# Attention scores from zero-padded keys, earlier loads and another order at the start of a kernel

## The chip, the cores and the metric

The kernel runs on one core of one Trainium2 chip. The metric is the device time of one launch in microseconds; the median of three runs is given. One further execution was taken with the hardware profiler, and all rows below come from it. PE is TensorE (PEld its weight loads), DVE is VectorE, ACT is ScalarE, POOL is GpSimd, SP is SyncE, which issues nearly all of the DMAs.

## The reference

Attention in chunks is followed by two MLPs. All is float32.

```
for each chunk c of 32 queries (768 per sequence, 4 x 8 heads of size 64):
    keys = 8 memory keys + keys from 16 to the left to 8 to the right of the chunk
    a = softmax(q_c @ keys.T / 8);  out_c = a @ values        # 8 memory values likewise
x = out as (3072 tokens, 512)
h = x @ w_in;  g = where(h > 0, h, exp(min(h, 0)) - 1);  x = g @ w_out       # 512 -> 2048 -> 512
h = x @ w_in2; g = s * max(h, 0)**2 + b;                 out = g @ w_out2
```

## The kernel before

**Units.** Attention is cut into 24 units of 128 queries (4 chunks of 32) with all 8 heads. A unit loads `k` (512 KB, 128 partitions: rows 0 to 63 are the head dimension of one head of a pair, rows 64 to 127 that of the other), `q` (256 KB, laid out alike) and `v` (512 KB). A unit goes through these steps, named by a letter:

- S (`scores`, line 233): for each of 4 head pairs, 4 chunks and 2 heads one product of 64 rows, 32 columns of `q` against 64 keys of its head: 32 products, which the profile shows as 64 instructions, since each float32 product is issued twice. The two heads write two PSUM banks.
- M: on DVE the row maximum and the subtraction (lines 258, 259). E: the exponential on ACT (line 261). G: on DVE the sum, its reciprocal and the scaling (lines 263 to 266).
- P: four transposes on PE (line 281). T: their copy to `pt` on ACT (line 204).
- V (`values`, line 305): 32 products, shown as 64 instructions. X (`to_x`, line 317): ACT writes the rounded result to `xh` (line 204) and DVE the remainder to `xl` (line 208).

**MLP weights.** A chunk `raw` of w1 (512 KB) is loaded (line 149) and goes through four steps "w": ACT `top` (line 158), DVE `t` (line 161), ACT high part (line 172), DVE low part (line 208).

**The order at the start.** `EARLY` (line 39) is an order written out by hand for units 0 to 3 and the scores of unit 4. Each word is one step: S, M, E, G, P, T, V, X with the unit's number; `k` and `v` load a unit's `k` with `q`, or `v`; `l` loads a weight chunk; `w` is the next weight step; `d` are products without use; `h00` to `h11` are the first two halves of the products of weight chunks 0 and 1 with units 0 and 1. `keep` (line 130) chains the instructions of each engine in this order, so an engine does not pass over one that waits. SP issues its DMAs in program order too. After `EARLY` the main loop goes through the weight chunks, with the first MLP's products and the remaining attention units beside them; its first products (`h1`, line 386) need X of units 2 and 3.

**Memory.** `q`, `k` and `v` have two buffers each (`stg`, line 180), so the load of unit 2 waits until unit 0 has been used, and the load of unit 3 for unit 1. Scores of units 0 to 4 go through one pair of PSUM banks (`ps_a`, line 109).

Of the kernel before, what the change touches and what calls it, by code (L numbers as in the profile page):

```python
# [8 lines left out]
F32 = mybir.dt.float32  # L9
# [8 lines left out]
PSUM = bass.MemoryType.PSUM  # L18


B, H, S, D, NMEM = 4, 8, 768, 64, 8
CH, LEFT, RIGHT = 32, 16, 8
P = 128
DM, DFF, NT = H * D, 2048, B * S
KT, NF = DM // P, DFF // P
U = 4 * CH
# [3 lines left out]
NP = H // 2  # L30
# [6 lines left out]
NTOP = 1  # L37
LEAD = 4
EARLY = """
k1 l v0 k2 v1 k3 S0 M0 E0 d8 S1 G0 d2 P0 M1 w T0 w E1 S2 V0 w G1 l v2 k4 P1 M2 w X0 T1 E2 V1 G2 X1 S3 l v3 k5  # L40
P2 M3 w T2 w E3 h00 V2 w G3 h01 w X2 P3 l v4 T3 S4 h10 V3 w M4 E4 h11 w X3 G4 w w
"""
ORDER = (1, 2, 6, 5, 7, 3, 4)
BANK = {1: 1, 2: 2, 6: 1, 5: 5, 7: 1, 3: 5, 4: 1}
# [1 line left out]
NC, NCK = U // CH, LEFT + CH + RIGHT + NMEM  # L46
QC, KC, VC = NP * U, NC * NCK, NP * NC * D
# [14 lines left out]
def tile_attention_then_two_mlps(ctx, tc, q_in, k_in, v_in, w1, w2, s_in, b_in, out):  # L62
# [17 lines left out]
    nc = tc.nc  # L80
# [4 lines left out]
    def engine(step):  # L85
# [14 lines left out]
    wps = [ctx.enter_context(tc.tile_pool(name="wpi", bufs=1, side="right")),  # L100
           mctx.enter_context(tc.tile_pool(name="wpo", bufs=1))]
# [3 lines left out]
    xp = ctx.enter_context(tc.tile_pool(name="xp", bufs=1, side="right"))  # L105
# [4 lines left out]
    vctx = ExitStack()  # L110
    ps_v = vctx.enter_context(tc.tile_pool(name="ps_v", bufs=1, space=PSUM))
    xctx = ExitStack()
    ps_x = xctx.enter_context(tc.tile_pool(name="ps_x", bufs=1, space=PSUM))
    ps_acc = []

    y_dram = dp.tile([P, KT, NT], F32, name="y_dram")
# [13 lines left out]
    def keep(ins):  # L130

        if keeping[0]:
            e = ins.ins.engine
            if e in last:
                tc.add_manual_dep(ins.ins, last[e].ins.name,
                                  mybir.DependencyInfo(mybir.DependencyClass.NoSync, mybir.DependencyReason.DATA))
            last[e] = ins
        return ins
# [41 lines left out]
    stg = actx.enter_context(tc.tile_pool(name="stg", bufs=2))  # L180
# [6 lines left out]

    QK, V = {}, {}

    def load_qk(u):  # L190
        kb = stg.tile([P, NP, KC], F32, tag="k", name="kb")
        nc.sync.dma_start(out=kb, in_=k_in[u])
        q = stg.tile([P, QC], F32, tag="q", name="q")
        nc.sync.dma_start(out=q, in_=q_in[u])
        QK[u] = (q, kb)

    def load_v(u):
        V[u] = stg.tile([P, VC], F32, tag="v", name="v")
        nc.sync.dma_start(out=V[u], in_=v_in[u])

    def hi_copy(key, hi, src):
# [14 lines left out]
    def two_banks(nm):  # L216


        pool = ps_v if phase[0] == 0 and nm == "V" else ps_a
        return pool.tile([P, 2, 512], F32, tag="a", name="ps" + nm)  # L220
# [5 lines left out]
    def own_keys(u):  # L226

        return sms[u % 2].rearrange("p r z n -> p z r n")

    def by_halves(a):  # L230
        return a.rearrange("p (z r) -> p z r", z=2).unsqueeze(3).to_broadcast([U, 2, NP, NCK])

    def scores(u, ps):
        q, kb = QK[u]
        for r in range(NP):
            for c in range(NC):
                for z in range(2):
                    o, rows = slice(c * CH, (c + 1) * CH), slice(z * D, (z + 1) * D)
                    mm = keep(nc.tensor.matmul(ps[o, z, r * NCK:(r + 1) * NCK],
                                               q[rows, r * U + c * CH:r * U + (c + 1) * CH],  # L240
                                               kb[rows, r, c * NCK:(c + 1) * NCK], start=True, stop=True))
        return mm
# [5 lines left out]

    def softmax_steps(u, ps):

        src = ps[:, :, :NP * NCK].rearrange("p z (r n) -> p z r n", r=NP)
        sm, j = own_keys(u), u % UPB
        if j == 0:
            keep(nc.vector.memset(src[:CH, :, :, NMEM:NMEM + LEFT], NEG))
        if j == UPB - 1:
            keep(nc.vector.memset(src[U - CH:, :, :, NCK - RIGHT:], NEG))
        nmx, sums, rs = (ap2.tile([U, H], F32, tag=nm, name=nm) for nm in ("nmx", "sums", "rs"))
        keep(nc.vector.tensor_reduce(out=nmx.rearrange("p (z r) -> p z r", z=2), in_=src, op=ALU.max, axis=AX.X))
        keep(nc.vector.tensor_tensor(out=sm, in0=src, in1=by_halves(nmx), op=ALU.subtract))
        yield  # L260
        keep(nc.scalar.activation(out=sm, in_=sm, func=AF.Exp, scale=SCALE))
        yield
        keep(nc.vector.tensor_reduce(out=sums.rearrange("p (z r) -> p z r", z=2), in_=sm, op=ALU.add, axis=AX.X))
        keep(nc.vector.tensor_scalar(out=rs, in0=sums, scalar1=1e-9, scalar2=None, op0=ALU.add))
        keep(nc.vector.reciprocal(out=rs, in_=rs))
        keep(nc.vector.tensor_tensor(out=sm, in0=sm, in1=by_halves(rs), op=ALU.mult))
        yield

    def step_S(u):

        ps = two_banks("S")
        scores(u, ps)
        softmax(u, ps)

    def step_P(u):

        sm = sms[u % 2]
        if u < NU0:
            ps = (ps_h if ps_acc else ps_x).tile([P, 512], F32, tag="h", name="psP")
            for r in range(NP):  # L280
                keep(nc.tensor.transpose(ps[:, r * U:(r + 1) * U], sm[:, r].rearrange("p z n -> p (z n)"), ident))
            if keeping[0]:
                return ps
            return to_pt(ps)
        for c in range(NC):
            rows = slice(c * CH, (c + 1) * CH)
            for k in range(P // CH):
                z, n0 = divmod(k * CH, NCK)
                nc.vector.transpose(out=pt[k * CH:(k + 1) * CH, :, rows], in_=sm[rows, :, z, n0:n0 + CH])  # L289

    def to_pt(ps):

        keep(hi_copy("pt", pt, ps.rearrange("p (r n) -> p r n", r=NP)))
# [11 lines left out]
    def values(u, ps):  # L305
        v = V[u]
        for i in range(NP // 2):
            for c in range(NC):
                cs, o = slice(c * CH, (c + 1) * CH), 256 + i * U + c * CH
                for r in (2 * i, 2 * i + 1):  # L310
                    for z in range(2):
                        rows = slice(z * D, (z + 1) * D)
                        keep(nc.tensor.matmul(ps[r % 2 * D:(r % 2 + 1) * D, z, o:o + CH],  # L313
                                              v[rows, (r * NC + c) * D:(r * NC + c + 1) * D], pt[rows, r, cs],
                                              start=True, stop=True))

    def to_x(u, ps, behind=None):

        t, jj = tile_of[u]
        po = ps[:, :, 256:].rearrange("p z (i n) -> p z i n", i=NP // 2)  # L320
        if t < 2:
            if t not in X:
                X[t] = x_tiles(t)
            xh, xl = (x.rearrange("p (i z) n -> p z i n", z=2)[:, :, :, jj * U:(jj + 1) * U] for x in X[t])
            ins = keep(hi_copy("xh", xh, po)), keep(sub(xl, po, xh))
        else:
            xs = xsp.tile([P, KT, U], F32, tag="xs", name="xs")
            ins = (hi_copy("xh", xs.rearrange("p (i z) n -> p z i n", z=2), po),)
            nc.sync.dma_start(out=x_dram[:, :, u * U:(u + 1) * U], in_=xs)
        for i in ins if behind else ():  # L330
            wait(i, behind)
# [165 lines left out]
    load_qk(0)  # L497
    wraw = {}
    nc.vector.memset(pt, 1.0)
    for top in tops:  # L500
        nc.gpsimd.memset(top, 0)

# [34 lines left out]
    def weights_to(w, n, ahead):  # L537

        while wnext[0] < min(n, MICRO * NF):
            k, m = divmod(wnext[0], MICRO // 2)  # L540
            load_ws(w, k + 1 + ahead)
            if m == 0:
                wsteps[:] = [split_w(*SLOTS[k], wraw[k])]
            next(wsteps[0])
            wnext[0] += 1

    SM, PSV, PSP = {}, {}, {}

    def early(what):

        op_, n = what[0], int(what[1:] or 0)
        if op_ == "S":
            ps = two_banks("S")
            scores(n, ps)
            SM[n] = softmax_steps(n, ps)
        elif op_ in "MEG":
            next(SM[n])
        elif op_ == "P":
            PSP[n] = step_P(n)
        elif op_ == "T":  # L560
            to_pt(PSP.pop(n))
        elif op_ == "V":
            PSV[n] = two_banks("V")
            values(n, PSV[n])
        elif op_ == "X":
            to_x(n, PSV.pop(n))
        elif op_ == "w":
            weights_to(w1, wnext[0] + 1, 0)
        elif op_ == "d":
            warm(n)  # L570
        elif op_ == "h":
            h_half(*divmod(n, 10))
        elif op_ == "k":
            load_qk(n)
        elif op_ == "v":
            load_v(n)
        elif op_ == "l":
            load_ws(w1, wload[0] + 1)
# [167 lines left out]
    z = NTILE1 % 2  # L746
# [167 lines left out]
```

## Time and profile before

| | us |
|---|---|
| median of 3 runs | 1074.35 (1073.3 to 1074.74) |
| the profiled execution | 1074.13 |
| its span, first to last instruction | 1072.3 |

| engine | busy us | share of the span |
|---|---|---|
| PE | 1055.4 | 98% |
| PEld | 860.1 | 80% |
| DVE | 733.4 | 68% |
| ACT | 546.7 | 51% |
| POOL | 1.2 | 0% |

A matmul's end is modelled, so a busy PE need not be PE at its peak. The chain of waits is followed back from the last instruction; "issue" in it is time in which an engine waited for nothing that the profile shows. [...]

### The profile page before, as it was taken

The page shows a single profiled execution, that of the slowest core. Times are in us where ns is not written, and L with a number is a line of the kernel's source. Part 1 is how long each engine was busy: PE and PEld are TensorE (multiplying, and loading weights), DVE is VectorE, ACT ScalarE, POOL GpSimd, SP SyncE. Part 2 cuts the span into 40 slices and gives each one's busy share as a digit, 9 for nine tenths or more (in the row PEclk, how much of TensorE's full clock was granted, in tenths as well). Part 3 has the DMA queues.
Part 4 walks back from the last instruction along what each step waited for, and adds up shares of the span by engine and source line. Part 5 has one row for each costly group of instructions (what it writes and reads, how often), then busy time and mean ns, then how long its engine had stood idle before and what let it go on. Part 6 is the DMA issues. An engine that isn't in the chain of part 4 may idle for free.

```text
span 1072.3 us, 18728 instructions
## 1 busy us (share of the span) xinstructions
PE 1055.4 (98%) x7466; PEld 860.1 (80%) x7466; DVE 733.4 (68%) x1135; ACT 546.7 (51%) x771; POOL 1.2 (0%) x7
## 2 busy tenths in 40 slices
PE   7999999999999999999999999999999999999998
PEld 6778888888788888888888787788888788888886
DVE  6898677787777768778772356696266795375854
ACT  3777532434334367767653355654355653355542
POOL 0000000000000000000000000000000000000000
PEclk8999999999999999999999999999999999999999
DMA  8964214535234169988912566777766777766773
GB/s 322 394 259 193 92 60 135 174 104 177 73 119 143 37 208 341 343 329 322 330 59 79 170 192 188 230 213 234 233 190 188 243 214 232 210 189 195 204 201 126
DMA packets 94838, 213.02 MB, mean 199 GB/s; under 512 B 9760, under 2 KB 17952, under 8 KB 92704
## 3 DMA queue, kind: packets, MB, share of 16 engines
q1 hardware_dynamic: 94176, 210.79, 60.9%
q8 instruction: 59, 0.97, 0.4%
q10 hardware_dynamic: 576, 1.05, 0.3%
q14 instruction: 27, 0.22, 0.1%
HBM read 164.61 MB, written 47.19 MB: 198 GB/s over the span
## 4 chain that ended last, share of the span: by engine, by line
PE 83%; DVE 7%; DMA 5%; ACT 3%; issue 2%; SPq 0%; ACTq 0%; DVEq 0%
PE psH L361 14%; PE psH L363 13%; PE psH L362 13%; PE psL L362 7%; PE psL L363 7%; PE acc L361 6%; PE psL L361 6%; PE acc L362 6%; PE acc L363 6%; DMA hi<-y_dram 2%; DVE pt L289 2%; DMA xl<-x_dram 1%; DVE g L394 1%; PE psVS L313 1%; PE psV L313 1%
## 5 line engine op out<-in xcount | busy, mean ns | idle before, releaser
L361 PE MATMUL psH<-xh,w 128*128 128x512 f32 (+1 forms) x392 | 153.8, 392 | 0.8 <-DVE g L394 0.7
L362 PE MATMUL psH<-xl,w 128*128 128x512 f32 (+1 forms) x392 | 151.3, 386 | 0.6 <-issue 0.6
L363 PE MATMUL psH<-xh,w 128*128 128x512 f32 (+1 forms) x392 | 151.8, 387 | 0.0
L361 PE MATMUL acc<-gh,w 128*128 128x512 f32 x384 | 151.5, 395 | 0.0
L362 PE MATMUL acc<-gl,w 128*128 128x512 f32 x384 | 150.3, 391 | 0.0
L363 PE MATMUL acc<-gh,w 128*128 128x512 f32 x384 | 149.9, 390 | 0.0
L392 ACT ACTIVATE g<-psH 128x512 f32<-128x512 f32 x96 | 56.9, 593 | 99.6 <-PE psH L363 60.4
L394 DVE SCALAR_TENSOR_TENSOR g<-g,psH 128x512 f32<-128x512 f32 x96 | 65.7, 685 | 59.7 <-ACT g L393 58.5
L204 ACT ACTIVATE gh<-g 128x512 fp32r<-128x512 f32 x96 | 60.3, 628 | 77.7 <-DVE g L394 77.5
L361 PE MATMUL psH<-hi,hi 128*128 128x512 f32 x240 | 93.7, 397 | 0.8 <-ACT p L765 0.6
L363 PE MATMUL psH<-hi,hi 128*128 128x512 f32 x240 | 93.6, 390 | 0.0
L362 PE MATMUL psH<-hi,hi 128*128 128x512 f32 x240 | 93.5, 390 | 0.0
L815 ACT ACTIVATE g2xl<-g 128x1024 fp32r<-128x1024 f32 x56 | 59.5, 1062 | 60.1 <-PE psL L363 59.9
L362 PE MATMUL psL<-g2l,hi 128*128 128x512 f32 x224 | 87.4, 390 | 0.8 <-DVE g2l L208 0.7
L361 PE MATMUL psL<-g2xl,hi 128*128 128x512 f32 x224 | 86.9, 390 | 0.8 <-ACT g2xl L815 0.8
L361 PEld LDWEIGHTS psH<-xh,w 128*128 128x128 f32 x392 | 73.9, 188 | 17.0 <-DVE g L394 1.3
L363 PE MATMUL psL<-g2xl,hi 128*128 128x512 f32 x224 | 87.1, 389 | 0.0
L208 DVE TENSOR_TENSOR gl<-g,gh 128x512 fp32r<-128x512 f32 x96 | 66.2, 689 | 30.6 <-ACT gh L204 29.1
L362 PEld LDWEIGHTS psH<-xl,w 128*128 128x128 f32 x392 | 73.9, 189 | 16.0 <-issue 0.9
L363 PEld LDWEIGHTS psH<-xh,w 128*128 128x128 f32 x392 | 73.9, 188 | 15.5
L361 PEld LDWEIGHTS acc<-gh,w 128*128 128x128 f32 x384 | 72.1, 188 | 16.1
L363 PEld LDWEIGHTS acc<-gh,w 128*128 128x128 f32 x384 | 72.1, 188 | 15.6
(108 smaller groups left out, 1840.7 us busy)
## 6 DMA issues: line engine op xcount, KB each, us to landing
hi<-s_dram SPq DMA_DIRECT2D x336, 256.0 KB, 3.0
raw<-w SPq DMA_DIRECT2D x64, 511.8 KB, 6.3
s_dram<-right SPq DMA_DIRECT2D x16, 1024.0 KB, 5.1
kb<-k SPq DMA_DIRECT2D x24, 512.0 KB, 5.7
v<-v SPq DMA_DIRECT2D x24, 512.0 KB, 4.2
s_dram<-left SPq DMA_DIRECT2D x16, 768.0 KB, 4.1
q<-q SPq DMA_DIRECT2D x24, 256.0 KB, 5.2
out<-r SPq DMA_DIRECT2D x24, 256.0 KB, 3.7
```

The costliest lines, as they stand in the source:

```text
L204: return nc.scalar.activation(out=hi, in_=src, func=AF.Copy)
L208: return nc.vector.tensor_tensor(out=lo, in0=src, in1=f(hi), op=ALU.subtract)
L289: nc.vector.transpose(out=pt[k * CH:(k + 1) * CH, :, rows], in_=sm[rows, :, z, n0:n0 + CH])
L313: keep(nc.tensor.matmul(ps[r % 2 * D:(r % 2 + 1) * D, z, o:o + CH], v[rows, (r * NC + c) * D:(r * NC + c + 1) * D], pt[rows, r, cs], start ...
L361: keep(nc.tensor.matmul(o, sa(a[0]), sb(b[0]), start=first, stop=False, skip_group_check=again))
L362: keep(nc.tensor.matmul(o, sa(a[0]), sb(b[1]), start=False, stop=False, skip_group_check=again))
L363: return keep(nc.tensor.matmul(o, sa(a[1]), sb(b[0]), start=False, stop=last, skip_group_check=again))
L392: nc.scalar.activation(out=g[:, :n], in_=ps[:, :n], func=AF.Relu, scale=-1.0)
L394: nc.vector.scalar_tensor_tensor(out=g[:, :n], in0=g[:, :n], scalar=-1.0, in1=ps[:, :n], op0=ALU.add, op1=ALU.max)
L815: nc.scalar.activation(out=gh, in_=g[:, block], func=AF.Copy)
```

## The change

For units 0 to 3 the keys lie in a tile `WIDE` of twice the size: in its first half only the rows of the first head hold keys and the rows of the second are zero, in its second half the other way round. One product of 128 rows and 32 columns of `q` then gives both heads' scores, 128 columns wide: 16 products a unit instead of 32. The zeros are written once, by DVE for units 0 and 1 and by POOL for units 2 and 3, and `k` is loaded with two DMAs of 64 partitions (256 KB) each. `WIDE` uses the memory that `xh` and `xl` take later; `q` and `v` of units 2 and 3 use that of the last two weight chunks. Units 0 to 4 no longer share buffers of `k`; only `q` and `v` of units 4 and 5 (and `k` from unit 6 on) reuse earlier ones. The scores of units 0 to 3 alternate between two single banks. `EARLY` loads nearly everything first, has another order of steps, no `d`, and `k5 v4` at its end; both orders have 12 steps "w".

```diff
 EARLY = """
-k1 l v0 k2 v1 k3 S0 M0 E0 d8 S1 G0 d2 P0 M1 w T0 w E1 S2 V0 w G1 l v2 k4 P1 M2 w X0 T1 E2 V1 G2 X1 S3 l v3 k5
-P2 M3 w T2 w E3 h00 V2 w G3 h01 w X2 P3 l v4 T3 S4 h10 V3 w M4 E4 h11 w X3 G4 w w
+k1 v0 k2 l v1 k3 l v2 l v3 k4 S0 M0 E0 S1 G0 P0 M1 T0 S2 E1 w M2 V0 E2 G1 X0 P1 G2 T1 S3 w V1 X1 P2 T2 w M3
+V2 w X2 E3 h00 h01 w G3 S4 P3 w T3 w V3 w M4 h10 h11 w X3 E4 w G4 w w k5 v4
 """
...
-    ps_x = xctx.enter_context(tc.tile_pool(name="ps_x", bufs=1, space=PSUM))
+    ps_x, ps_s = (xctx.enter_context(tc.tile_pool(name=nm, bufs=1, space=PSUM)) for nm in ("ps_x", "ps_s"))
...
+    def lend(i, c, shape, name):
+
+        return wps[i].tile(shape, F32, tag=f"w{i}_{c}", name=name)
+
+    WIDE = [xp.tile([P, 2, NP, KC], F32, tag=tag, name=f"wide{u}") for u, tag in enumerate(("xh0", "xl0", "xh1", "xl1"))]
+
     def load_qk(u):
-        kb = stg.tile([P, NP, KC], F32, tag="k", name="kb")
-        nc.sync.dma_start(out=kb, in_=k_in[u])
-        q = stg.tile([P, QC], F32, tag="q", name="q")
+        if u < len(WIDE):
+            kb = WIDE[u]
+            for z in range(2):
+                rows = slice(z * D, (z + 1) * D)
+                nc.sync.dma_start(out=kb[rows, z], in_=k_in[u, rows])
+        else:
+            kb = stg.tile([P, NP, KC], F32, tag="k", name="kb")
+            nc.sync.dma_start(out=kb, in_=k_in[u])
+        q = lend(0, NF + 1 - u, [P, QC], "q") if u in (2, 3) else stg.tile([P, QC], F32, tag="q", name="q")
...
-        V[u] = stg.tile([P, VC], F32, tag="v", name="v")
+        V[u] = lend(1, NF + 1 - u, [P, VC], "v") if u in (2, 3) else stg.tile([P, VC], F32, tag="v", name="v")
...
+        if u < len(WIDE):
+            for r in range(NP):
+                for c in range(NC):
+                    mm = keep(nc.tensor.matmul(ps[c * CH:(c + 1) * CH, 2 * r * NCK:2 * (r + 1) * NCK],
+                                               q[:, r * U + c * CH:r * U + (c + 1) * CH],
+                                               kb[:, :, r, c * NCK:(c + 1) * NCK], start=True, stop=True))
+            return mm
...
+    for u, kb in enumerate(WIDE):
+        for z in range(2):
+            (nc.vector if u < 2 else nc.gpsimd).memset(kb[(1 - z) * D:(2 - z) * D, z], 0.0)
...
-            ps = two_banks("S")
+            if n == 0:
+                SB[:] = [two_banks("S")[:, 0], ps_s.tile([P, 512], F32, tag="s", name="psS")]
+            ps = SB[n % 2] if n < len(WIDE) else two_banks("S")
```

## Rows read from the trace of the kernel before

**Rows 1.** Busy time by stretch: span, PE, PEld, DVE, ACT, POOL, clock, DMA share, GB/s.

```profile
10.00:13.00 3.00, 0.65 (x4) 0.42 (x4) 2.83 (x6) 2.12 (x4) 0.00 (x0) 1.00 1.04 414
14.00:23.00 9.00, 8.18 (x215) 7.25 (x206) 7.08 (x13) 3.60 (x7) 0.00 (x0) 0.50 0.90 324
24.00:33.00 9.00, 6.96 (x226) 5.98 (x219) 5.44 (x11) 4.12 (x8) 0.00 (x0) 1.00 1.01 382
40.00:60.00 20.00, 20.00 (x327) 15.82 (x326) 18.39 (x35) 16.42 (x30) 0.00 (x0) 1.00 0.80 302
```

**Rows 2.** The chain of waits, 0 to 40 us: start, us, what.

```profile
6.88 6.10 DMA q<-q
...
13.11 1.05 PE psS L239 x58
...
16.41 1.06 PE psP L281 x4
...
18.20 1.93 PE psV L313 x48
...
29.19 1.62 issue
```

**Rows 3.** SP's queue, 0 to 40 us: whom its issues waited for.

```profile
SPq L199 <- PE psV L313: 11.8, 4, 5.3
```

**Rows 4.** DMA issues, one each, at 1.64, 6.88 and 9.86 us: time to landing.

```profile
kb<-k SPq DMA_DIRECT2D x1, 512.0 KB, 6.2
...
q<-q SPq DMA_DIRECT2D x1, 256.0 KB, 6.1
...
q<-q SPq DMA_DIRECT2D x1, 256.0 KB, 6.6
```

**Rows 5.** PE's scores at 20.06 us, by shape, at half clock: mean ns.

```profile
L239 PE MATMUL psS<-kb,q 64*32 64x64 f32 x64 | 1.2, 310 | 0.0
```

**Rows 6.** Timeline: scores at either clock; transposes and values at full clock.

```profile
20.06 1.18 PE L239 MATMUL psS<-kb,q 64*32 64x64 f32 x64
...
26.19 0.60 PE L281 MATMUL psP<-ident,sm 128*128 128x128 f32 x4
...
26.73 0.86 PE L239 MATMUL psS<-kb,q 64*32 64x64 f32 x64
...
41.01 1.14 PE L313 MATMUL psV<-pt,v 64*64 64x32 f32 x64
```

**Rows 7.** Timeline of DVE: one M, one G, and what follows next.

```profile
14.53 0.68 DVE L258 TENSOR_REDUCE nmx<-psS 128x8 f32<-128x512 f32 x1
15.25 0.69 DVE L259 TENSOR_TENSOR sm<-psS,nmx 128x512 f32<-128x512 f32 x1
...
23.55 0.69 DVE L263 TENSOR_REDUCE sums<-sm 128x8 f32<-128x512 f32 x1
24.27 0.17 DVE L264 TENSOR_SCALAR rs<-sums 128x8 f32<-128x8 f32 x1
24.47 0.20 DVE L265 RECIPROCAL rs<-rs 128x8 f32<-128x8 f32 x1
24.71 0.69 DVE L266 TENSOR_TENSOR sm<-sm,rs 128x512 f32<-128x512 f32 x1
25.32 0.69 DVE L208 TENSOR_TENSOR w<-t,w 128x512 fp32r<-128x512 f32 x1
```

**Rows 8.** Timeline of DVE: X of unit 3, the last before `h1`.

```profile
32.14 0.69 DVE L208 TENSOR_TENSOR xl<-psV,xh 128x512 fp32r<-128x512 f32 x1 [2.50 <-ACT xh L204]
```

**Rows 9.** ACT and DVE to 37 us, and POOL to 40 us, by shape: mean ns.

```profile
L172 ACT ACTIVATE w<-t 128x512 fp32r<-128x512 f32 x4 | 2.5, 630 | 0.8 <-DVE t L161 0.8
L204 ACT ACTIVATE xh<-psV 128x512 fp32r<-128x512 f32 x4 | 2.4, 598 | 7.8 <-PE psV L313 7.8
...
L499 DVE MEMSET pt<- 128x512 f32 x1 | 0.5, 485 | 0.9 <-PEq L897 0.9
...
L501 POOL MEMSET top<- 128x512 int32 x1 | 0.5, 524 | 0.3 <-POOLq L897 0.3
```

More of the change, by code (lines that the diff above doesn't have):

```diff
@@ L228, in own_keys, with score_view @@
         return sms[u % 2].rearrange("p r z n -> p z r n")
+    def score_view(u, ps):
+        if u < len(WIDE):
+            return ps.rearrange("p (r z n) -> p z r n", r=NP, z=2)
+        return ps[:, :, :NP * NCK].rearrange("p z (r n) -> p z r n", r=NP)
     def by_halves(a):
@@ L234, in scores @@
         q, kb = QK[u]
+        if u < len(WIDE):
+            for r in range(NP):
[4 more added lines that the diff above has]
+            return mm
         for r in range(NP):
@@ L249, in softmax_steps @@
     def softmax_steps(u, ps):
-        src = ps[:, :, :NP * NCK].rearrange("p z (r n) -> p z r n", r=NP)
+        src = score_view(u, ps)
         sm, j = own_keys(u), u % UPB
@@ L545, in weights_to @@
             wnext[0] += 1
-    SM, PSV, PSP = {}, {}, {}
+    SM, PSV, PSP, SB = {}, {}, {}, []
     def early(what):
```

## The prediction

> **What bounds the kernel now.** I read the windows first, then the chain of waits, then the queues and the single steps. In the windows PE is busy in all of the 20 us from 40 to 60, at the full clock [rows 1]; before that it is not: 8.18 of 9 us at half the clock from 14 to 23, and 6.96 of 9 from 24 to 33, where DVE too has only 5.44. So the main loop is bound by PE, and the stretch to about 33 us by a chain of single steps. A microsecond won or lost there moves everything behind it, and the change touches nothing else.
>
> The chain shows which steps [rows 2]. It waits for `q` of unit 2, which lands at 6.88 + 6.10 = 12.98 us. From 13.11 PE goes without a pause through S2, V0, P1, V1 and S3, at half the clock: in the three microseconds before, it had been busy for 0.65 [rows 1]. The clock is back in the row that begins at 24 us. After that come V2, S4 and V3, with a stall of 1.62 us put down to "issue", and at 32.14 us DVE's X of unit 3 [rows 8], for which `h1` waits. I take this X3 as the mark at which the main loop starts, and compare the new start with it.
>
> The loads hold a second limit. SP's issues of `v` waited 11.8 us in all for V steps [rows 3], as buffers came free late. Yet the DMA engines were hardly idle: shares of 1.04 and 1.01 of their time, with 0.90 between [rows 1]. At 414 GB/s a load of 512 KB (524,288 bytes) takes 1.27 us and one of 256 KB 0.63.
>
> **The change part by part.**
>
> *Loads ahead, in memory of their own.* Before `q` of unit 2 stand k0, q0, k1, q1, w0, v0 and k2; in the new order w0 stands behind it. At unchanged rates it lands 1.27 us sooner, at 11.71. `q` of unit 3 has the same loads before it as now, and lands at 9.86 + 6.6 = 16.5 [rows 4]. The new copies of `v` no longer wait for V0 and V1, but S2 to V3 are not waiting for `v` now either. Moving `k5 v4` to the end costs nothing while SP issues far ahead: 19 DMAs precede k5, none of them held up by PE beyond S0.
>
> *`k` in two halves of 64 partitions.* The trace has no such load. From below, a half costs by its bytes, 0.63 us, and the pair 1.27 as now. From above, it costs by the bytes in each partition: the loads of `k` and `w` have 4 KB per partition and take 1.27 us, those of `q` 2 KB and take 0.63, and all cover 128 partitions, so these rows fit either reading. A half has 4 KB per partition; its nearest row is a whole load of `k`, and by that the pair takes 2.54 us. I take this end: 1.27 us more for each of k0 to k3. `q` of unit 2 then lands at 11.71 + 3 x 1.27 = 15.52, that of unit 3 at 16.5 + 4 x 1.27 = 21.6.
>
> [...]
>
> *Scores.* S of 64 instructions takes 1.18 us at half the clock and 0.86 at the full one [rows 6], and one instruction 0.31 [rows 5]; so 0.87 of the 1.18 is the streaming of 64 columns, eight products side by side (two halves of rows, four of columns). From below, the new S is half of the instructions at the same spacing: 0.44 + 0.31 = 0.75. From above, each of its 32 instructions fills all rows, so four stand side by side instead of eight, and each streams 128 columns: 2 x 0.87 + 0.31 = 2.05 at half the clock, 1.4 at full. I take the upper end, since the half clock made the rows longer and they are therefore partly bound by streaming.
>
> *Clock.* The `d` products go. PE then has only S0, S1 and P0 before S2, less than it had before the clock fell; I take half the clock from S2 through V1, as now. Full clock is the third case below.
>
> *Zeros.* Each memset is 64 partitions x 1024 elements. 512 elements took 0.485 us on DVE and 0.524 on POOL [rows 9], so at twice that, four on DVE take 3.9 us after `pt`, to about 5.3 us, and four on POOL 4.2. DVE has no other work before S0's scores; POOL's `ident` is ready near 6 us and is wanted by P0 beyond 11. Cost 0. If a memset waited for a load of the other half, S0 would come about 1 us later and still be ahead of S2's data.
>
> *Single banks for S0 to S3* free S1 from M0; S1 waits for its data anyway: 0.
>
> **The sum.** Handover between engines is 0.04 us. DVE's M takes 0.72 + 0.60 until the next instruction can start, its G 0.72 + 0.21 + 0.24 + 0.69 = 1.86 to its result, and each other step 0.60 [rows 7].
>
> S2 runs 15.6 to 17.65. M2 from 17.7; G1 starts at 19.02 and ends at 20.88. P1 (1.06) [rows 2] to 22.0, T1 (0.60) [rows 9] to 22.65. S3 has its data at 21.6 and ends on PE at 23.75; V1 follows it there from 23.45 with 1.93 [rows 2], to 25.4. ACT's part of X1 to 26.0, DVE's from 26.05. From here it is DVE: X1 0.60, M3 1.32, w 0.60, X2 0.60 with 0.2 waited for ACT, G3 1.86, to 31.25. Then P3 0.60 [rows 6], T3 0.60, ACT's weight step 0.63 [rows 9] and four handovers, to 33.2; w 0.60 and M4 1.32; X3 at 35.15. Before it was 32.14, so the start is 3.0 us longer.
>
> V2 from 27.0 (1.14) [rows 6] and V3 from 32.6 end before DVE needs them. k4 and q4 land near 28.6, S4 comes at 30.1. The DVE work left behind X3 is the same but for one weight step, which the old order had in the main loop at this place. The sum is 1074.13 + 3.0 = 1077.1 us. The profiled execution lies 0.2 us below the median of the runs, well inside their spread, so I add nothing.
>
> What is not in it: the issue stall of 1.62 us, which may come again (+1.6) or not; the clock coming back before V1 (-1.3); the main loop taking a little back, as the weight loads keep their distance.
>
> **The rivals.**
>
> *No change: the halves load at the full rate, but PE is slow.* `q` of unit 2 at 11.71; S0 ends some 0.6 us later than now, so P0 comes at 11.4 and at half the clock S2 runs 12.4 to 14.4. G1 to 17.6, P1 to 18.7, S3 to 20.6, V1 to 22.3, X1 on DVE at 22.95, and 9.1 us on (35.15 - 26.05) X3 at 32.05: 0.1 us sooner, 1074.0. For it: the engines already run at a share of 1.0, so the bytes may be all that counts. What the earlier keys win is spent on wider scores and on G1, now behind M2.
>
> *Faster: full rate and full clock.* S2 ends at 12.95, G1 at 16.2, P1 16.8, S3 17.95, V1 18.85, X1 on DVE 19.5, X3 9.1 us on at 28.6: 3.5 us sooner, 1070.6. For it: the work is reordered to keep DVE going, 256 of PE's early instructions fewer can be late, and S near its lower end would save 0.9 more a unit. Against it: PE had more to do when the clock fell than it will have. It decides whether S2 starts before 13 us and PE is at the full clock there.
>
> *Much slower: column groups not side by side,* or loads waiting for memsets: 32 instructions of 0.21 us at half the clock, 6.8 us a unit, some 5 us more in each of S2 and S3: above 1084. The eight side by side of today speak against it.
>
> **How the numbers follow.** My case has a chance of 0.47, with its own range 1075.4 to 1079.4: at the low end the clock back by V1 and a weaker loss of rate, at the high end the issue stall too. No change has 0.25, spread by 1.5 us to either side; faster 0.25; much slower 0.03. A difference below 0.2%, 2.1 us, can't be told from none here. Slower: 0.8 x 0.47 + 0.1 x 0.25 + 0.03 + 0.01 = 0.44; faster: 0.15 x 0.25 + 0.95 x 0.25 = 0.28; the same: 0.28. The range takes in all but the last case and the ends of the others: 1070.6 to 1079.4.
>
> **What would show it.** In the changed trace: S2's first product at 15.0 us or later, waiting for a DMA, shows the halves at half the rate; 13 or earlier shows the forecast wrong. S of units 2 and 3 near 2 us at clock 0.50 or 1.4 at 1.00 shows the streaming; below 0.9 shows fewer instructions to be what counts. DVE's X of unit 3 near 35 us shows the sum; near 32 the first rival, near 28.6 the second. The busy time of PE from 40 us on should be the same, only shifted; if it has more idle time there, the main loop has moved too and the sum lacks a term.

## The result: 1082.7 us, 0.7% slower, and the profile after

The changed kernel takes 1082.72 us in the median of six runs (1079.06 to 1086.17), the kernel before 1074.55 beside it (1073.3 to 1077.63): a ratio of 1.0073, with a 95% interval of 1.0048 to 1.0098. The forecast was 1077.1 with a range to 1079.4: the sign is right, and 8 us is about three times the loss that was forecast. The profiled execution took 1081.47 us (span 1079.7), 7.34 above that of before, so the rows below have the whole loss to explain.

PE's busy time is what it was, 1055.4 us before and

```profile
PE 1055.7 (98%) x7328; PEld 860.5 (80%) x7328; DVE 737.6 (68%) x1139; ACT 546.7 (51%) x771; POOL 4.9 (0%) x11
```

after (the page's busy times by engine), so what was lost is, in sum, idle time of PE. The windows of the changed kernel come next, with the columns of [rows 1] (the clock is the granted share of full speed, the DMA share that of the core's 16 DMA engines):

```profile
10.00:13.00 3.00, 2.33 (x36) 1.80 (x27) 2.65 (x6) 0.18 (x1) 0.00 (x0) 0.50 1.07 239
14.00:23.00 9.00, 7.36 (x178) 6.09 (x180) 5.91 (x12) 2.95 (x5) 0.00 (x0) 0.54 1.04 345
24.00:33.00 9.00, 5.60 (x197) 4.67 (x196) 6.64 (x12) 4.81 (x9) 0.00 (x0) 1.00 1.03 403
36.00:40.00 4.00, 4.00 (x44) 3.47 (x47) 3.81 (x8) 1.44 (x3) 0.00 (x0) 0.57 1.04 409
40.00:60.00 20.00, 20.00 (x315) 16.33 (x316) 18.23 (x35) 17.17 (x31) 0.00 (x0) 1.00 0.83 306
```

Of before, one stretch does not stand in [rows 1]:

```profile
36.00:40.00 4.00, 3.32 (x19) 2.49 (x18) 3.86 (x8) 3.10 (x7) 0.00 (x0) 1.00 1.02 403
```

From 24 to 33 us PE is busy for 5.60 us instead of 6.96, and from 36 to 40 it works at little more than half the clock. From 40 to 60 it is busy without a gap at the full clock, as before. The DMA engines' share is 1.03 or more in the four rows up to 40 us; before, there was a gap from 14 to 23 (0.90) [rows 1]. The chain of waits of the start (start, us, what) says where PE stood:

```profile
5.42 8.07 DMA wide<-k
...
14.13 1.97 PE psS L256 x32
...
20.53 1.87 PE psS L256 x32
...
27.45 0.83 issue
...
32.40 2.17 issue
...
46.52 0.43 PE acc L386
```

S2 starts at 14.13 instead of 13.11 [rows 2] and is 1.97 us long. Then come two stalls that wait for no data, 0.83 and 2.17 us. The chain of before had two as well up to there, 1.62 us [rows 2] and one of 0.42 at 24.61, so they are 1.0 us longer in sum. The main loop's first product that adds to `acc`, the sums of the first MLP's second product, runs at 46.52 us; in the chain of before the same product, on its line 361, stands at 42.14. On DVE, the X of unit 3 is at 35.66 instead of 32.14 [rows 8]:

```profile
35.66 0.69 DVE L220 TENSOR_TENSOR xl<-psV,xh 128x512 fp32r<-128x512 f32 x1 [1.75 <-ACT xh L216]
```

A second loss lies 560 us later, where the first MLP ends and the second begins. The chain there, after:

```profile
607.37 0.25 PE acc L388
607.64 0.70 DVE big L448
608.36 5.25 DMA y_dram<-big
613.69 0.61 ACT m L795
614.34 0.50 PE psH L386
```

and before:

```profile
602.57 0.25 PE acc L363
602.85 0.70 DVE big L423
603.57 3.10 DMA y_dram<-big
606.75 0.61 ACT m L765
607.40 0.50 PE psH L361
```

The last product of the first MLP comes 4.80 us later than before. PE goes on with products of the second MLP, until one has to wait for ACT's copy `m`, which itself waits for the last store of the first MLP's result. That product comes 6.94 us later, the store takes 5.25 us instead of 3.10, and PE stands for 2.86 us instead of 0.71 (in brackets; first after, then before):

```profile
614.34 0.50 PE L386 MATMUL psH<-xc,hi 128*128 128x512 f32 x1 [2.86 <-ACT m L795]
607.40 0.50 PE L361 MATMUL psH<-xc,hi 128*128 128x512 f32 x1 [0.71 <-ACT m L765]
```

What stands beside that store is seen in SP's queue (start, us): the load of a block `yr`, a part of the first MLP's result that is read back for the second, after

```profile
607.40 0.37 SPq L658 DMA_DIRECT2D yr<-y_dram  x1
```

and before

```profile
599.88 0.37 SPq L628 DMA_DIRECT2D yr<-y_dram  x1
```

After, it starts at the last product's end, one microsecond ahead of the last store; before, 3.7 us ahead of it. So 7.34 us are: 3.52 to X3, 0.9 more to the first `acc` product (clock 0.57 from 36 to 40), 0.4 in the main loop, 2.1 at the boundary and 0.4 behind it.

### The profile page after: what moved, and what is told of

Same layout as the page of the kernel before. It is cut to its first block, busy times and chain, and to the rows that moved or that the text cites. A ratio compares the mean times of both kernels' runs of the same rounds, so it can differ in the third digit from the quotient of the medians.

```text
span 1079.7 us, 18458 instructions
## 1 busy us (share of the span) xinstructions
PE 1055.7 (98%) x7328; PEld 860.5 (80%) x7328; DVE 737.6 (68%) x1139; ACT 546.7 (51%) x771; POOL 4.9 (0%) x11
## 4 chain that ended last, share of the span: by engine, by line
PE 81%; DVE 8%; DMA 5%; ACT 3%; issue 2%; SPq 1%; ACTq 0%; DVEq 0%
PE psH L386 13%; PE psH L388 13%; PE psH L387 13%; PE psL L387 7%; PE acc L386 7%; PE psL L388 7%; PE acc L388 6%; PE acc L387 6%; PE psL L386 6%; DMA hi<-y_dram 2%; DVE pt L314 2%; DMA xl<-x_dram 1%; PE psVS L338 1%; DMA x_dram<-xs 1%; DVE g L419 1%
## 5 line engine op out<-in xcount | busy, mean ns | idle before, releaser
L386 PEld LDWEIGHTS psH<-xh,w 128*128 128x128 f32 x392 | 74.1, 189 | 17.5 <-DVE g L419 1.3
L388 PEld LDWEIGHTS acc<-gh,w 128*128 128x128 f32 x384 | 72.1, 188 | 15.7
```

The lines of the kernel that those rows point to most:

```text
L386: keep(nc.tensor.matmul(o, sa(a[0]), sb(b[0]), start=first, stop=False, skip_group_check=again))
L388: return keep(nc.tensor.matmul(o, sa(a[1]), sb(b[0]), start=False, stop=last, skip_group_check=again))
```

## The experiments

Times are medians, each beside runs of before on the same chip, whose median lay between 1074.5 and 1075.1 every time; a ratio is to those runs. My first theory was that the halves of `k` set the start and that the rest is a consequence; its rivals were the new order, the wide products, and the loads issued ahead.

**The changed kernel, one part undone.** Whole loads: `k` goes into the first half in one DMA of 128 partitions, and the second half is all zero; the scores of units 0 to 3 are therefore not the reference's.

```diff
-            for z in range(2):
-                rows = slice(z * D, (z + 1) * D)
-                nc.sync.dma_start(out=kb[rows, z], in_=k_in[u, rows])
+            nc.sync.dma_start(out=kb[:, 0], in_=k_in[u])
```

> The changed kernel, but k of units 0 to 3 comes in one DMA of 128 partitions, whole, into the first half of the padded tile; the second half is all zeros (so the scores of these units are sums over both heads and not the reference's; all sizes, products and memsets stay). Theory 1, a half costs by its bytes per partition and this delays the start: k lands in 1.3 us instead of 2.3 to 2.6, q of unit 2 near 10.5 us instead of 14.04, S2 starts near 11 instead of 14.13, X3 near 32.6 instead of 35.66, time 3 us below the changed kernel, near 1079.5. Theory 2, PE decides (wide scores at half the clock, its stalls): X3 at 35 or later, time within 1 us of the changed kernel.

Measured: 1078.24 (1.0032, interval 1.0017 to 1.0047), 4.5 less than with halves. S2 starts at 12.10 and X3 stands at 31.93, 0.2 us ahead of before, and yet 3 us are lost: the chain has the last store at 5.04 us here too. The halves cost something, and they are not all.

Narrow products from whole keys, with the new order, the own memory and the loads ahead left in:

```diff
-    WIDE = [xp.tile([P, 2, NP, KC], F32, tag=tag, name=f"wide{u}") for u, tag in enumerate(("xh0", "xl0", "xh1", "xl1"))]
+    WIDE = [xp.tile([P, NP, KC], F32, tag=tag, name=f"wide{u}") for u, tag in enumerate(("xh0", "xl0", "xh1", "xl1"))]
...
-                nc.sync.dma_start(out=kb[rows, z], in_=k_in[u, rows])
+            nc.sync.dma_start(out=kb, in_=k_in[u])
...
-                                               kb[:, :, r, c * NCK:(c + 1) * NCK], start=True, stop=True))
```

> The new order and the memory of their own, but scores as before (64 rows, 64 columns, two banks) from whole keys, without zeros. Theory 1 and wide scores together are the cause: q of unit 2 near 10.5 us, S 1.1 to 1.2 us instead of 1.93 at half the clock, X3 near 30.8, time 4 to 5 us below the changed kernel and at or below the kernel before (1073 to 1075). Rival, the new order itself costs (G1 behind M2, X1 ahead of M3, no warming products): X3 at 33 or later and time 1077 or more.

Measured: 1078.39 (1.0038, 1.0023 to 1.0053), as with wide products from whole keys, where the first theory asked for 1073 to 1075. X3 at 34.63, with a stall of 1.45 us at 19.69, and the last store at 5.19 us. Wide or narrow makes no difference that shows; what is left is the order or the loads ahead.

The old order of loads and steps, `d` products included, with all else as changed:

```diff
-k1 v0 k2 l v1 k3 l v2 l v3 k4 S0 M0 E0 S1 G0 P0 M1 T0 S2 E1 w M2 V0 E2 G1 X0 P1 G2 T1 S3 w V1 X1 P2 T2 w M3
-V2 w X2 E3 h00 h01 w G3 S4 P3 w T3 w V3 w M4 h10 h11 w X3 E4 w G4 w w k5 v4
+k1 l v0 k2 v1 k3 S0 M0 E0 d8 S1 G0 d2 P0 M1 w T0 w E1 S2 V0 w G1 l v2 k4 P1 M2 w X0 T1 E2 V1 G2 X1 S3 l v3 k5
+P2 M3 w T2 w E3 h00 V2 w G3 h01 w X2 P3 l v4 T3 S4 h10 V3 w M4 E4 h11 w X3 G4 w w
```

> The changed kernel with the order of the kernel before (its warming products too): halves, zeros, wide scores and own memory stay. Theory 1 with wide scores: q of unit 2 (w0 ahead of it again) near 15.3 us, S2 near 15.4, X3 at 35.5 to 37, time 1081 to 1084. Rival, the order is the cause: X3 near 33, time 1076 or less.

Measured: 1082.72 (1.009, 1.006 to 1.012), the time of the changed kernel. Its stalls named "issue" are longer, 2.44, 0.82 and 2.35 us, X3 is at 37.09, and the last store takes 5.18 us. With the halves and the loads ahead in place, the new order is not what costs. With memory of their own the loads of units 2 and 3 wait for no V step in the old order either.

Narrow products in the old order of steps, with memory of their own and the new order of loads:

```diff
-k1 l v0 k2 v1 k3 S0 M0 E0 d8 S1 G0 d2 P0 M1 w T0 w E1 S2 V0 w G1 l v2 k4 P1 M2 w X0 T1 E2 V1 G2 X1 S3 l v3 k5
-P2 M3 w T2 w E3 h00 V2 w G3 h01 w X2 P3 l v4 T3 S4 h10 V3 w M4 E4 h11 w X3 G4 w w
+k1 v0 k2 l v1 k3 l v2 l v3 k4 S0 M0 E0 d8 S1 G0 d2 P0 M1 w T0 w E1 S2 V0 w G1 P1 M2 w X0 T1 E2 V1 G2 X1 S3
+P2 M3 w T2 w E3 h00 V2 w G3 h01 w X2 P3 T3 S4 h10 V3 w M4 E4 h11 w X3 G4 w w k5 v4
```

> The kernel before with q, k and v in memory of their own and the new order of the loads alone: the old order of the steps, scores as before, whole keys. If only the arrival of q of unit 2 counts: S2 starts near 11.8 instead of 13.11, X3 near 30.8 instead of 32.14, time 1073.2. If PE's chain at half the clock and its issue stalls take that back: X3 at 32 or later, time 1074 to 1076.

Measured: 1079.07 (1.0037, 1.0021 to 1.0053), above both expectations. It proves little by itself: `w0` comes later in that order, and a step "w" that stands ahead of T0 waits for it. Its last store takes 3.75 us, though, and not 5; that led to the next question.

**The boundary of the two MLPs.** The first MLP multiplies its activations in two parts, rounded and remainder; `gl` is the remainder, one for each weight chunk. In the built programs the block `yr` of the late load shares its memory with `gl` buffers. In the kernel before, the last `gl` on it is that of the last chunk but one; in the changed kernel the last two `gl` have changed places, and it is that of the last chunk. The traces show no addresses, but they show the wait: SP's load waits for products into `acc` (us, times, longest), after up to the last one at 607.37 us and before up to one at 599.85:

```profile
SPq L658 <- PE acc L388: 6.7, 1, 6.7
```

```profile
SPq L628 <- PE acc L362: 7.1, 1, 7.1
```

Exchanging two of the four `yr` buffers undoes that in the changed kernel and brings it about in the kernel before; reversing all four frees the load early. The edit of the first two, and of the third:

```diff
+    p2["yr"] = [p2["yr"][k] for k in (1, 0, 2, 3)]
```

```diff
+    p2["yr"] = [p2["yr"][k] for k in (3, 2, 1, 0)]
```

> The changed kernel with one edit far from it: of the four memory slots that the second MLP's block loads use, the first load takes the second slot, so it follows the last-but-one gl again, as in the kernel before, and not the last. Slot theory: the load is issued near 2.8 us sooner against PE's last acc product, ahead of the y_dram stores; the last store lands in 3.1 us instead of 5.25; the loss between acc and psL (2.8 us in the profiles) goes and the time falls by 2 to 3 us, to 1080. Rival, that gap is chance of one run: no change, 1082 to 1083.

> The kernel before with the same exchange, which there puts the first block load behind the last gl, where the changed kernel has it. Slot theory: the load leaves 2.8 us later, between the stores, the last store takes 5 us or more, and the time grows by 2 to 3 us, to 1077. Rival, chance: no change, 1074 to 1075.5.

> The kernel before with the four slots in reverse, so that the first block load takes one that is free long before. Slot theory: the load leaves before 597 us, the stores have the DMA engines to themselves and the last lands in 2 to 2.5 us instead of 3.1: 0.5 to 1 us faster than before. Rival: the store is not what ends the wait there; no change.

Measured: the changed kernel falls to 1080.55 (1.0044, 1.0029 to 1.0058), by 2.2 us (the interval of the changed kernel, 1.0048 to 1.0098, overlaps this one); the kernel before rises to 1077.59 (1.0021, 1.0010 to 1.0032), by 3.1, and that is clear of noise. The load and the last store in the kernel before with exchanged buffers, from SP's queue and from the chain:

```profile
601.64 0.37 SPq L628 DMA_DIRECT2D yr<-y_dram  x1
```

```profile
602.60 5.07 DMA y_dram<-big
```

and the store in the changed kernel with exchanged buffers, whose load starts at 601.90, 3.7 us ahead:

```profile
605.59 3.28 DMA y_dram<-big
```

From both sides, then: a load issued a microsecond ahead of the last store makes it some 2 us longer, and PE waits for it: 2.69 us in the kernel before with exchanged buffers, 0.90 in the changed kernel with them. Over all kernels here the store took 5.04 to 5.25 us with the load 1.0 us ahead (five), and 3.10 to 4.18 with the load 3.7 us ahead (eleven). Reversing all four, with the load at 594.64, gave 1074.67 (0.9995, 0.9984 to 1.0005): no gain that shows, where I had expected half a microsecond or more. In its trace PE no longer waits there, but that wait was only 0.71 us, less than the interval can tell.

**Loads ahead.** The kernel before, with keys of units 0 to 3 and queries and values of units 2 and 3 in their own memory, and all loads of `EARLY` placed ahead of S0; steps, products and `yr` as before:

```diff
-k1 l v0 k2 v1 k3 S0 M0 E0 d8 S1 G0 d2 P0 M1 w T0 w E1 S2 V0 w G1 l v2 k4 P1 M2 w X0 T1 E2 V1 G2 X1 S3 l v3 k5
-P2 M3 w T2 w E3 h00 V2 w G3 h01 w X2 P3 l v4 T3 S4 h10 V3 w M4 E4 h11 w X3 G4 w w
+k1 l v0 k2 v1 k3 l v2 k4 l v3 k5 l v4 S0 M0 E0 d8 S1 G0 d2 P0 M1 w T0 w E1 S2 V0 w G1 P1 M2 w X0 T1 E2 V1 G2 X1 S3
+P2 M3 w T2 w E3 h00 V2 w G3 h01 w X2 P3 T3 S4 h10 V3 w M4 E4 h11 w X3 G4 w w
```

> The kernel before, its order of steps and its order of loads, scores as before from whole keys, but q, k and v in memory of their own and all loads of the hand-written order issued at its start. q of unit 2 lands at 13 us as before, so nothing is late for lack of data. If only arrival counts: X3 near 32, time 1073.5 to 1075. Fetch theory, PE's stalls named issue are its instruction fetches held up by queued loads: with the queue always full the stalls before X3 come to 3 us or more instead of 2.0, time 1076 to 1078.

Measured: 1078.43 (1.0036, 1.0019 to 1.0052), four microseconds lost, though no load up to 37 us lands later than it did. Then the same kernel with its `v` in the old staging buffers and the old place of the loads, so that SP waits for V steps again:

```diff
-        V[u] = lend(1, NF + 1 - u, [P, VC], "v") if u in (2, 3) else stg.tile([P, VC], F32, tag="v", name="v")
+        V[u] = stg.tile([P, VC], F32, tag="v", name="v")
```

> Before with keys of units 0 to 3 and queries of units 2 and 3 in memory of their own, but every `v` in the old staging buffers and the loads in the old order: the loads of `v` wait for V steps again, so SP can't put the whole start ahead of the engines' code. Queue theory (a full load queue delays the code that PE fetches): issue stalls of PE at the start add to 2.6 us or less, the time is 1074 to 1076. Rival (the place in memory itself costs, or chance of the order): 1078 to 1079, as with all loads ahead.

Measured: 1074.68 (0.9998, 0.9986 to 1.0009): the loss is gone. The memory itself costs nothing; issuing without a wait does. The window from 14 to 23 us with loads ahead (columns as in [rows 1]):

```profile
14.00:23.00 9.00, 7.27 (x201) 6.27 (x200) 6.23 (x12) 2.99 (x5) 0.00 (x0) 0.53 1.03 406
```

and with `v` waiting:

```profile
14.00:23.00 9.00, 8.19 (x268) 7.35 (x269) 6.20 (x12) 3.10 (x6) 0.00 (x0) 0.53 0.75 266
```

At the same clock PE gets 67 products less done while the DMA engines are full. Its stalls named "issue" to 42 us add to 4.69 us with loads ahead (0.56, 0.42, 1.50, 0.80, 1.41) and to 2.54 with `v` waiting (1.24, 0.45, 0.85). The first `acc` product stands at 45.52 and at 41.96 us: 2.15 of these 3.56 us are stalls. The rest is not separated; the clock was 0.76 against 1.00 from 24 to 33 us.

**What PE waits for in these stalls.** The theory by now: its own code, which comes in packets through the DMA engines (the profile of before has a queue of kind "instruction" with 59 packets and 0.97 MB, q8), behind the loads. The rival: the stalls belong to the queue or to the data, whatever the number of instructions. The test gives PE 256 more instructions that need nothing new: the products of S1 issued three times, where PE waits for `q` of unit 2 anyway; under loads ahead, and with `v` waiting.

```diff
-            scores(n, ps)
+            for _ in range(3 if n == 1 else 1):
+                scores(n, ps)
```

> Before's order of steps with every load issued ahead (as in the variant with loads alone, 1078.43), and the products of S1 issued three times: 256 of PE's instructions more, at some 1.2 us for each 128, at a place where PE waits for q of unit 2 anyway. Code theory (with a full load queue PE's code comes only every 6.3 us, so each 256 instructions more must be waited for): 2 to 6 us slower than 1078.43, at 1080.5 or more, with issue stalls of over 5 us in all before 40 us. Rival (the stalls depend on the queue and not on how many instructions PE has): 1078 to 1079.5.

> The same with the loads of `v` waiting for V steps as before (1074.68 without the added products). Code theory: the queue leaves room for code, so the 256 instructions cost less here than in the variant with loads ahead: 1074.5 to 1076. If PE's added time is itself on the path: the same loss in both.

Measured: 1080.77 with loads ahead (1.0067, 1.0043 to 1.0092), 2.3 more than without the added products, and 1079.87 with `v` waiting (1.0048, 1.0030 to 1.0066), 5.2 more. The first is where the code theory had it, with 8.1 us of issue stalls (its interval overlaps that without the added products, but all six runs lie above the rival's 1079.5); the second is a miss by 4 us. The chains tell why. With loads ahead:

```profile
8.11 1.64 PE psS L253 x97
9.74 4.33 issue
14.07 0.74 PE psS L253 x46
```

with `v` waiting:

```profile
8.37 1.64 PE psS L253 x97
10.00 4.98 issue
14.99 1.06 PE psS L253 x48
```

In both, PE stops for more than 4 us between two products of the third copy of S1, whose keys and queries it has just used twice. What it lacks, then, is most likely the next instruction. The table of DMA queues has one packet of code between 11.5 and 12.9 us in the first of them, none from 9 to 11.5 and none from 13 to 17.5, among loads that fill the engines:

```profile
q1 hardware_dynamic: 157, 0.56, 99.7%
q8 instruction: 1, 0.02, 4.8%
```

The places of the stalls say the same, and more strongly. In all kernels here PE has 37 stalls of 0.4 us or more before 44 us that are named "issue", and each stands after 218 to 222, 345 to 348, 472 to 475, 600 to 602, 727 or 728, or 855 of PE's products, whatever these products are, whenever they come and whatever the order of steps. Five windows from 0 us to the end of a stall (PE's products are in the first bracket, its weight loads in the second; the clock does not matter here): the kernel before (stall of 1.62 us), the changed kernel (2.17), loads ahead (1.50), narrow products in the new order (0.44), loads ahead with S1 three times (4.33):

```profile
0.00:30.80 30.80, 22.71 (x600) 18.45 (x601) 19.37 (x36) 11.74 (x18) 1.16 (x7) 0.83 0.90 330
0.00:34.55 34.55, 21.84 (x472) 17.11 (x472) 22.14 (x39) 10.80 (x17) 4.88 (x11) 0.80 0.97 315
0.00:27.06 27.06, 17.84 (x474) 14.50 (x474) 16.79 (x32) 9.14 (x14) 1.16 (x7) 0.81 0.95 362
0.00:33.52 33.52, 23.68 (x600) 19.35 (x600) 17.55 (x34) 10.82 (x17) 1.17 (x7) 1.00 0.95 361
0.00:14.06 14.06, 6.95 (x222) 5.44 (x222) 3.78 (x8) 2.69 (x3) 1.17 (x7) 1.00 0.86 321
```

These places are 126 to 128 products apart, with their weight loads some 254 instructions, and each of the 37 stalls ends 2.3 to 2.7 us after a packet of that queue. The queue is PE's: it has 59 packets in the whole kernel before, 253 of PE's 14,932 instructions for each, 60 with the 256 added, and 58 in the changed kernel. With all loads ahead its packets come at 12.3, 18.3, 24.6 and 31.0 us; with `v` waiting they come at 11.7, 15.9, 23.3 and 28.0.

So it is the code that is late. And the stall falls before 15 us, while the first loads fill the engines in both kernels (their share is 102.8% from 9 to 11.5 us with loads ahead and 103.4% from 10 to 12.2 with `v` waiting): waiting `v` steps help only behind it. That was the miss.

**The changed kernel with causes removed.** Buffers exchanged, `v` in the staging buffers, its loads behind V0 and V1; once with the halves and once with whole loads (scores as in the first experiment):

```diff
-k1 v0 k2 l v1 k3 l v2 l v3 k4 S0 M0 E0 S1 G0 P0 M1 T0 S2 E1 w M2 V0 E2 G1 X0 P1 G2 T1 S3 w V1 X1 P2 T2 w M3
+k1 v0 k2 l v1 k3 S0 M0 E0 S1 G0 P0 M1 T0 S2 E1 w M2 V0 l v2 k4 E2 G1 X0 P1 G2 T1 S3 w V1 l v3 X1 P2 T2 w M3
...
+    p2["yr"] = [p2["yr"][k] for k in (1, 0, 2, 3)]
```

> After with the two yr buffers exchanged, `v` in the staging buffers and `l v2 k4` behind V0, `l v3` behind V1; the halves of `k` stay. Queue theory: 1 to 3 us below the same kernel with all loads ahead (1080.55): 1077.5 to 1079.5, fewer or shorter issue stalls before 36 us. Rival (the halves alone fill the queue until 21 us, so the late code stays late): no change, 1080 to 1081.

> After with whole loads of `k` (scores of units 0 to 3 not the reference's), the two yr buffers exchanged, `v` in the staging buffers and `l v2 k4` behind V0, `l v3` behind V1. If the three causes (halves 4.5, buffer 2 to 3, queue 2 to 4 us) add up: 1078.2 - 2.5 - 2 = 1073 to 1075, X of unit 3 near 31. If what is saved at the start is lost again to a late `v` or to the clock: 1076 or more.

Measured: 1077.87 with halves (1.0028, 1.0016 to 1.0040), 2.7 below the kernel with exchanged buffers alone, as the theory had it. By the ratios it is 1.7 us, and the two intervals overlap; its profile still has stalls of 0.63 and 1.40 us and a DMA share of 1.03 from 14 to 23 us. So this step rests on the times alone, and its size is open. With whole loads 1076.61 (1.0015, 0.9999 to 1.0031), above the 1073 to 1075 of three causes that add up. They do not: whole loads were worth 4.5 us at first, clear of noise, and 1.3 here, which can't be told from none.

**Two parts alone.** The kernel before without its ten `d` products, and the kernel before with wide products and single banks, from keys loaded whole with zeros in the second half (scores as above), `v` waiting:

```diff
-k1 l v0 k2 v1 k3 S0 M0 E0 d8 S1 G0 d2 P0 M1 w T0 w E1 S2 V0 w G1 l v2 k4 P1 M2 w X0 T1 E2 V1 G2 X1 S3 l v3 k5
+k1 l v0 k2 v1 k3 S0 M0 E0 S1 G0 P0 M1 w T0 w E1 S2 V0 w G1 l v2 k4 P1 M2 w X0 T1 E2 V1 G2 X1 S3 l v3 k5
```

```diff
+            for r in range(NP):
+                for c in range(NC):
+                    mm = keep(nc.tensor.matmul(ps[c * CH:(c + 1) * CH, 2 * r * NCK:2 * (r + 1) * NCK],
...
+            nc.sync.dma_start(out=kb[:, 0], in_=k_in[u])
```

> Before without the ten `d` products, nothing else changed. If they hold the clock up: PE at half clock from the start to some 24 us, S0 and S1 longer, but both wait for loads; time 1074 to 1075.5. If their absence only shifts the ends of the code blocks: the stalls lie elsewhere, 1073 to 1076, and the clock falls where it fell. A gain of over 1 us would show that they were in the way.

> Before's order of steps and loads, `v` waiting as before, keys of units 0 to 3 loaded whole into a first half with zeros in the second (their scores are not the reference's), and the wide products: the change's products without the halves, the loads ahead, the new order and the other buffer. My sum (streaming sets S: 0.8 us longer each for S2 and S3 at half the clock, code 256 instructions shorter): 1073.5 to 1076. If fewer instructions are worth what the code theory makes of them even with room in the queue: 1071 to 1073.5. If wide products cost more than they show: 1076 or more.

Measured: 1075.24 (0.9995, 0.9983 to 1.0008) and 1075.13 (0.9999, 0.9983 to 1.0015). Neither is worth anything that can be told from none. In the second, S at full clock is

```profile
13.34 1.08 PE psS L254 x32
```

and X3 stands at 31.14, 1.0 sooner than before; the median shows none of it.

## Why the prediction was wrong

**Halves of `k`: right.** `v` of unit 0 lands at 11.1 us in the changed kernel (issued at 4.42, 6.7 to landing), the halves of unit 2 at 12.3 (issued at 4.90, 7.4 to landing) and 13.49: the pair took some 2.4 us for 512 KB. I had taken 2.54, and 1.27 as the other end. No row of before gave a size for the "weaker loss of rate" at the low end of my range; the trace puts the pair 0.1 us below 2.54. The first rival, full rate, falls.

**Scores: right at half the clock.** 1.97 us there (2.05 forecast), and 1.08 at the full one, where 1.4 had been put down without a working. The 1.97 fits the estimate from streaming, 2 x 0.87 + 0.31; half the instructions alone would have given 0.75 at half the clock, by an estimate from the same rows ([rows 5], [rows 6]). The rival in which column groups don't run side by side, 6.8 us a unit, falls.

**Zeros, single banks, `d`: right** at nothing that shows. The `d` were taken out alone; zeros and banks only together with the wide products (1075.13). Each memset on DVE took 0.91 us, and the four on POOL 3.91:

```profile
1.67 0.91 DVE L527 MEMSET wide<- 64x1024 f32 x1 [0.27 <-issue]
```

```profile
0.73 3.91 POOL L527 MEMSET wide<- 64x1024 f32 x4 [0.29 <-POOLq L927]
```

**The sum to X3: its end right, its course not.** 35.66 came for 35.15. But S2 came 1.5 us sooner than forecast (14.13 for 15.6), as the halves were shorter than taken and the other loads earlier, V1 ran at the full clock, and X1 on DVE stood at 24.16 instead of 26.05. From there to X3 it took 11.5 us instead of 9.1, and the two stalls, 0.83 and 2.17 us, lie in it. That the end fits within 0.5 us is luck: errors of either sign cancelled. I had left the stalls out: "the issue stall of 1.62 us, which may come again (+1.6) or not". They were a term of the sum, put at nothing without a reason, and 3.0 us here.

**The step that failed first: loads ahead.** It had been priced as a gain of 1.27 us for `q` and as nothing for the rest, because `v` was not being waited for and SP issues far ahead. That asked only when data arrives. The waits of SP [rows 3] left the DMA engines a gap from 14 to 23 us, a share of 0.90 [rows 1], and packets of code came at 15.7 and 22.7 us; with all loads ahead they came at 18.3 and 24.6, and the stalls named "issue" to 42 us added to 4.69 us. In the kernel before, this alone costs 3.7 us (1078.43 against 1074.68).

**The second: "the change touches nothing else".** The edit at the start exchanged two `gl` buffers 560 us later, and with them the moment at which a load leaves. That costs 2.2 us (changed kernel) to 3.1 (kernel before). No row of before showed that; the sentence claimed it without one. Its sign was among those named, more idle time of PE behind 40 us: 2.86 us instead of 0.71. Which part of the edit exchanges the buffers is not shown: with narrow products the new order does it and the old one does not, but with halves and loads ahead the old order does it too.

**Clock: half right.** S2 and S3 ran at half the clock as forecast (1.97 and 1.87 us). V1 did not: it took 1.11 us, where 1.93 had been taken, which is the case "the clock coming back before V1" that the sum had left out. Behind the stall of 2.17 us the clock fell again, to 0.57 from 36 to 40. I put the 0.9 us between X3 and the first `acc` product down to that; no run separated it. Nor do stalls and clock simply add: in the profiled execution of the changed kernel with exchanged buffers no stall of over 0.2 us came, PE's steps took what they take at half the clock up to V2 (1.93 us at 25.62), and X3 stood at 35.30 all the same, the first `acc` product at 44.62. There the packets of code came at 18.9, 25.0 and 31.5 us, hardly sooner than in the changed kernel (19.7, 25.8, 32.0), but PE came later to where they were needed: its 472nd product ended at 33.87 us instead of 32.40.

Of the 8.2 us between the medians, 2.2 are the buffer, 2.7 the loads ahead as far as they can be undone, 1.3 the halves, in this order of removal. In each of the three steps the two intervals overlap, so these sizes are rough; the buffer and the loads ahead are clear of noise in the kernel before, and the halves where they go first (4.5). (They are differences between kernels whose runs of before differ by up to 0.4.) The last 1.7, between 1076.61 and the 1074.86 of before beside it, are not settled: the interval reaches 0.9999. In that profile PE had clock 0.50 from 14 to 23 us and 0.63 from 24 to 33, where before had 0.50 and 1.00 [rows 1]; whether the new order, with less work for PE early on, brings this about each time was not tried.

## What to carry to other kernels

A wait on a load queue can be useful: without it the kernel before, with keys in memory of their own, took 1078.43 us, with it 1074.68. Before taking one away, ask what else goes through the same DMA engines, an engine's own code above all, and count the instructions of an unrolled start in blocks (some 254 here). The 37 stalls named "issue" here all stood at the same few places in PE's products, and each ended 2.3 to 2.7 us after a packet of code; such a stall belongs in the sum as a term, and with the loads of `v` waiting these stalls fell from 4.69 us to 2.54. After a change of allocation, compare the order of DMA issues at every later boundary with that of before, since a buffer that changes its last reader can move a load onto the path far from the edit, here 560 us behind it and for 2.2 to 3.1 us.

## What the runs showed that I had not expected

A load issued 1.0 us ahead of a store made the store 5.04 to 5.25 us long, where 3.7 us ahead left it at 3.10 to 4.18. And the times scatter: the changed kernel with exchanged buffers ran between 1075.62 and 1081.83 us, the kernel before beside it between 1072.64 and 1078.80. Its profiled execution was the shortest of ten, without any stall named "issue" of over 0.2 us before 40 us, so of that profile only the boundary and the comparison of stalls and clock were used. What the load does to the store inside the queues stays open; that the exchange of buffers sets it is shown from both sides.
